# Decode attention over a cached context: the order of the last loads, the softmax's rearrangement, and the placing of results

## The chip, the cores and the metric

The kernel runs on one core of a Trainium2 chip. The metric is the device time of one execution in microseconds: the median over several runs of the program without a profiler. A profiled execution stands beside it and has a time of its own.

## The reference

Everything is float32. The input `x` is 8 tokens (one for each of 8 batches) of 512 channels. It is normalised once, and two branches are added to it:

```
x  = A_x;  xn = layernorm(x)
q  = (xn @ wq) -> 32 query heads of 128        # wq 512 x 4096
k, v = caches [8 batches, 8 kv heads, 8192, 128]; 4 query heads share one kv head
A  = softmax(q k^T / sqrt(128)) v -> 4096 columns, @ wo      # wo 4096 x 512
u  = gelu(layernorm(xn)[b, d] * w1[f] + b1[f])               # f = 0..1791
B  = sum over f of u * w2[f], + b2
out = x + A + B
```

Each of the two caches holds 64 pairs of batch and kv head with 8192 x 128 numbers, 4 MiB a pair, so 512 MiB are read once and meet only 4 query rows each.

## The kernel before, in words

Work runs in 64 steps, `i = h * 8 + b`: kv head `h` outside, batch `b` inside. For every step one tile of keys and one of values is loaded, each 128 partitions x 64 rows x 128 channels (partition `p` holds the context rows `64p` to `64p + 63`). All loads go through one queue (SP, L86) into a ring of 5 such tiles (`RING`); a load is issued in `load_next`, called where a tile has been used up: after the scores of keys (`qk`, L261) and after the last part of values (`pv`, L337). The order of the loads is a list sorted by hand-made keys: keys of step `i` at `2i`, values of step `i` at `2(i + LAG) + 1` with `LAG = 2`. Near the end that gives keys 62, values 60, keys 63, values 61, values 62, values 63. The very last tile comes in six pieces.

The engines take their work in the order in which the program is written. The loop runs over `i`, and in one pass three steps are under way:

- keys `i` are turned in place by VectorE in four quarters (`turn_keys`, L247, 32 x 32 blocks);
- step `k = i - 1` has its scores made by TensorE (`qk`, L258) against `Z`, which holds the queries of one head, placed in blocks (`q_place`, L241; two copies of `Z`, filled by 14 copies on ScalarE), and then its softmax: row maximum (`sm_max`, L268), its spread to all partitions (`sm_spread`, L273), bias (`sm_bias`, L279), exponential with row sums (`sm_exp`, L285), 32 x 32 transposition (`sm_turn`, L291), the sum's reciprocal (`sm_sum`, L298 and L300), and seven matmuls of 64 columns with four ScalarE copies that put the probabilities as weights into `PT` (`sm_place`, L309 and L313);
- step `v = i - 2` multiplies its values with `PT` (`pv`, L327; four parts; 512 columns to a matmul, four strips of 32 output rows), two parts ahead of the softmax's end of step `k` and two behind it. The result is scaled on its way out of PSUM (L340), and one pass later `o_place` gathers it (L355 to L359; in the last head L363 and L365) into `OT`. The last step's values (`FINE`) go in matmuls of 128 columns (L333), so that each piece can start when it has landed.

After a head is complete, `o_project` multiplies with `wo` (L371) and adds to `yacc`, which is kept as four quarters of 32 partitions. The Mixer branch (`mx_begin`, `mx_step`, `mx_end`) runs beside it: for each batch 14 Gelus on ScalarE, with a product and a sum on GpSimd, two a pass in seven passes of every eight.

The rings in PSUM: `misc` has three buffers, the score and result tiles four, the Mixer one.

Of the kernel before, what the change touches and what calls it, by code (L numbers as in the profile page):

```python
# [15 lines left out]
REP = HQ // HKV  # L16
# [6 lines left out]
GT = CH_T // NB  # L23
# [7 lines left out]
ZW = (2 * NB - 1) * RB  # L31
NS = 2 * NB - 1
SL = CH_T * REP
FINE = N_IT - 1
LAG = 2
RING = 5
PAD = 384
# [3 lines left out]
def attn_mixer_kernel(ctx: ExitStack, tc: tile.TileContext, x, kc, vc, wq, wo, w1, b1, w2, b2, out):  # L41
# [7 lines left out]
    t2k = ctx.enter_context(tc.tile_pool(name="t2k", bufs=3))  # L49
# [17 lines left out]
    order.sort(key=lambda o: -o[0])  # L67
    WQ = []
# [8 lines left out]
    def load_next():  # L77
        if order:
            _, src, to, i = order.pop()
            h, b = divmod(i, B)  # L80
            t = ring.tile([P, NT, DH], F32, name="raw")
            rows = src[b, h].rearrange("(p t) d -> p t d", p=P)
            first, last = to is KR and not i, not order
            at = 0
            for n in (CH_T,) * NCH if first else (CH_T, CH_T, CH_T, 2 * GT, GT, GT) if last else (NT,):
                nc.sync.dma_start(t[:, at:at + n, :], rows[:, at:at + n, :])  # L86
                at += n
            to[i] = t
# [10 lines left out]
    x_sb = t2k.tile([B, D], F32, name="t2k")  # L99
# [4 lines left out]
    b2t = const.tile([B, 1], F32, name="b2t")  # L104
    yacc = const.tile([P, D // NB], F32, name="yacc")
    nc.vector.memset(yacc, 0.0)
# [13 lines left out]
    oh = const.tile([P, REP], F32, name="oh")  # L120
    nc.vector.tensor_reduce(oh, ident.rearrange("p (g h) -> p h g", h=REP), AX.X, ALU.add)
    ohw = t2k.tile([P, P], F32, name="t2k")
# [4 lines left out]
    oh32 = t2k.tile([P, W], F32, name="t2k")  # L127
# [3 lines left out]
    oh2 = work.tile([P, REP], F32, name="oh2")  # L131
# [5 lines left out]
    turn = const.tile([P, NS * W], F32, name="turn")  # L137
    for y in range(NS):
        o = -y % NB * W
        nc.vector.tensor_copy(turn[:, y * W:(y + 1) * W], ident[:, o:o + W])  # L140
# [15 lines left out]
    spread = const.tile([B, W], F32, name="spread")  # L156
    nc.vector.memset(spread, 0.0)
    nc.vector.tensor_copy(spread.rearrange("b (c s) -> b c s", s=BS)[:, :, 0], ident[:B, :B])
    Z = []
    for k in range(2):  # L160
        z = const.tile([P, NB, B, ZW], F32, name=f"z{k}")
        nc.gpsimd.memset(z, 0.0)
        Z.append(z)
    PT = []
    for k in range(2):
        t = const.tile([P, NCH * SL + W - REP], F32, name=f"pt{k}")
        nc.gpsimd.memset(t, 0.0)
        PT.append(t)
# [18 lines left out]
    xn = t2k.tile([B, D], F32, name="t2k")  # L187
    layer_norm(xn, x_sb)
    hn = one.tile([B, D], F32, name="g")
# [3 lines left out]
    xnT = one.tile([P, NC, W], F32, name="sq")  # L193
    nc.vector.memset(xnT, 0.0)
    hnT = const.tile([P, NC, B], F32, name="hnT")
# [4 lines left out]
    for c in range(NC):  # L200
        nc.tensor.transpose(m[:, P + c * B:P + (c + 1) * B], hn[:, c * P:(c + 1) * P], ident[:B, :B])
    nc.vector.tensor_copy(hnT, m[:, P:P + NC * B].rearrange("p (c b) -> p c b", b=B))
    m = misc()
    for j in range(NB):
        nc.tensor.matmul(m[j * W:(j + 1) * W, :D // NB], spread, yx[:, quarter[j]], start=True, stop=True)
    nc.vector.tensor_copy(yacc, m[:, :D // NB])
# [4 lines left out]
    def q_project():  # L211
        for a in range(2):
            m = misc()
            for g in range(HKV // 2):
                for c in range(NC):
# [7 lines left out]
            for g in range(HKV // 2):  # L223
                nc.tensor.transpose(mt[:, g * P:(g + 1) * P], q[:, g * DH:(g + 1) * DH], ident)
            nc.vector.tensor_copy(QT[:, a * HKV // 2:(a + 1) * HKV // 2].rearrange("p g b r -> p g r b"),
                                  mt.rearrange("p (g r b) -> p g r b", r=REP, b=W)[:, :, :, :B])
        WQ.clear()
        load_next()
        load_next()

    def q_place(h):
# [5 lines left out]
        dst = Z[h % 2].rearrange("p q b (s k r) -> p (q b) s k r", k=2, r=REP)  # L237
        for s in range(2 * NB - 1):
            a = slice(s % NB * W, (s % NB + 1) * W)
            for k in range(2):  # L240
                nc.scalar.copy(dst[a, :, s, k, :], src[a])  # L241
# [9 lines left out]
    def qk(i):  # L251
# [3 lines left out]
        for q in range(NB):  # L255
            for c in range(NCH):
                o = -c % NB * RB
                nc.tensor.matmul(S[i][c * W:(c + 1) * W, :].rearrange("p (t j) -> p t j", j=W),  # L258
                                 Z[h % 2][:, q, b, o:o + W], k[:, c * CH_T:(c + 1) * CH_T, q * W:(q + 1) * W],
# [16 lines left out]
    def sm_bias(i):  # L276
        t = one.tile([P, P], F32, name="sq")
# [3 lines left out]

    def sm_exp(i):
        p = big()
        lr = work.tile([P, 1], F32, name="lr")
# [3 lines left out]
    def sm_turn(i):  # L288
        p, lr = st[i]
        t = big()  # L290
        nc.vector.transpose(t, p)  # L291
        st[i] = (t, lr)

    RL = {}

    def sm_sum(i):
        m = misc()
        nc.tensor.matmul(m[:, :1], ohl, st[i][1], start=True, stop=True)  # L298
        rl = work.tile([P, 1], F32, name="rl")
        nc.vector.reciprocal(rl, m[:, :1])  # L300
        RL[i] = rl

    def sm_place(i):
        t = st.pop(i)[0].rearrange("p (t r x) -> p r t x", r=NB, x=RB)
        m = misc()
        for v in range(NS):
            r = v % NB
            o = -r % NB * W
            nc.tensor.matmul(m[:, v * SL:(v + 1) * SL].rearrange("p (t h) -> p t h", h=REP),  # L309
                             turn[:, o:o + P], t[:, r, :, :REP], start=True, stop=True)  # L310
        for a in range(NB):
            x = slice(a * W, (a + 1) * W)
            nc.scalar.copy(PT[i % 2][x, :NCH * SL], m[x, a * SL:(a + NCH) * SL])  # L313

# [3 lines left out]
    def pv(i, c):  # L318
        if not 0 <= i < N_IT:
            return  # L320
        if c == 0:
            O[i] = ps_a.tile([P, 512], F32, name="acc")
        v = VR[i][:, c * CH_T:(c + 1) * CH_T, :].rearrange("p t d -> p (t d)")
        for j in range(NB):
            o = (c * NB + j) * GT * REP
            if i < FINE:
                nc.tensor.matmul(O[i][j * W:(j + 1) * W, :], PT[i % 2][:, o:o + W], v[:, j * 512:(j + 1) * 512],  # L327
                                 start=(c == 0), stop=(c == NCH - 1))
                continue
            for u in range(GT):  # L330
                w = PT[i % 2][:, o + u * REP:o + u * REP + W]
                x = slice((j * GT + u) * DH, (j * GT + u + 1) * DH)
                nc.tensor.matmul(O[i][u * W:(u + 1) * W, :DH], w, v[:, x],  # L333
                                 start=(c == 0 and j == 0), stop=(c == NCH - 1 and j == NB - 1))
        if c == NCH - 1:
            del VR[i]
            load_next()  # L337
            w = 512 if i < FINE else DH
            ob = big()
            nc.scalar.activation(ob[:, :w], O.pop(i)[:, :w], AF.Copy, scale=RL.pop(i))  # L340
            OB[i] = ob
# [3 lines left out]
    def o_place(i):  # L345
        if not 0 <= i < N_IT:
            return
        h, b = divmod(i, B)
        if b == 0:
            OT[h] = OTS[h % 2]  # L350
        m = misc()
        ob = OB.pop(i)
        if h < HKV - 1:
            for u in range(GT):
                nc.tensor.matmul(m[:, :DH], pick[:, u, :], ob[:, u * DH:(u + 1) * DH],  # L355
                                 start=(u == 0), stop=(u == GT - 1))
            t = one.tile([P, P], F32, name="sq")
            nc.vector.tensor_tensor(t, m[:, :DH], keep, op=ALU.mult)
            nc.vector.tensor_reduce(OT[h][:, :, BS * b], t.rearrange("p (g c) -> p c g", c=REP), AX.X, ALU.add)  # L359
            return  # L360
        n = GT if i < FINE else 1
# [5 lines left out]
    def o_project(h):  # L367
        m = misc()
        for r in range(REP):
# [4 lines left out]


    mx = {}

    def mx_begin(b):
        hb = ps_h.tile([P, D], F32, name="hb")
        for c in range(NC):  # L380
            nc.tensor.matmul(hb[:, c * P:(c + 1) * P], hnT[:, c, b:b + 1].to_broadcast([P, P]), ident, start=True, stop=True)
# [11 lines left out]
    def mx_end(b):  # L393
        m = misc()
        for j in range(NB):
            nc.tensor.matmul(m[j * W:(j + 1) * W, :D // NB], bsel[:, BO - BS * b:BO - BS * b + W], mx[b][1][:, quarter[j]],
                             start=True, stop=True)
        nc.vector.tensor_add(yacc, m[:, :D // NB], yacc)
# [3 lines left out]
    q_place(0)  # L402
    for i in range(N_IT + LAG + 1):
        h, b = divmod(i, B)
        k, v = i - 1, i - LAG
        soft = 0 <= k < N_IT
        turn_keys(i, 0)
        o_place(v - 1)
        if soft:
            qk(k)  # L410
        turn_keys(i, 1)
        if soft:
            sm_max(k)
            sm_spread(k)
        if h and b == 0:
            mx_end(h - 1)
        if h < HKV:
            if b == 0:
                mx_begin(h)
            else:  # L420
                mx_step(h, 2 * (b - 1))
# [50 lines left out]
```

## Time and profile before

| | us |
|---|---|
| median of 3 runs | 1307.39 (1307.25 to 1311.2) |
| profiled execution | 1319.94 |
| its span in the trace | 1318.2 |
| PE busy | 939.2 (71%) |
| DVE busy | 728.1 (55%) |
| ACT busy | 463.5 (35%) |
| POOL busy | 232.2 (18%) |
| mean granted TensorE clock | 0.81 of full |

Busy times add up what an engine's instructions took; they overlap between engines. PE is TensorE with its matmuls, PEld its weight loads, DVE VectorE, ACT ScalarE, POOL GpSimd, SP the queue that issues the loads. A row of the groups names the line, the engine, the operation, what it writes and reads, the count, busy time and mean of one, and behind the bar the engine's idle time ahead of them with what ended it. One matmul in float32 leaves two records, so the 16 matmuls that multiply one step's values are 32 records.

### The profile page before, as it was taken

How to read it: one execution, taken by the hardware profiler on the slowest of the kernel's cores; microseconds unless marked ns; L12 is line 12 of the kernel's file. 1: busy time of each engine (PE TensorE's matmuls, PEld its weight loads, DVE VectorE, ACT ScalarE, POOL GpSimd, SP SyncE). 2: the span in 40 equal slices, each digit the busy share in tenths (PEclk: the TensorE clock that was granted, in tenths of full speed). 3: DMA queues.
4: the chain of work that ended last, by engine and by line, in shares of the span. 5: the costliest groups of instructions: out<-in, count | busy, mean ns of one | idle time of the engine just before them, and what ended most of it. 6: DMA issues, size and time to landing. Idle time of an engine off the chain costs nothing.

```text
span 1318.2 us, 15548 instructions
## 1 busy us (share of the span) xinstructions
PE 939.2 (71%) x6578; PEld 431.0 (33%) x6578; DVE 728.1 (55%) x751; ACT 463.5 (35%) x805; POOL 232.2 (18%) x248
## 2 busy tenths in 40 slices
PE   3677676786668677786667677687587677686777
PEld 3233233332233233342223233243243233233334
DVE  3765654655654646655655645655646645654530
ACT  0343333343334332343333433343323433333331
POOL 2111211221121211221111211111201221121210
PEclk9887897778886778778887877877868887887777
DMA  9999999999999999999999999999999999999990
GB/s 399 438 433 430 429 433 436 432 430 429 434 433 436 429 429 433 436 430 432 434 429 434 432 433 431 432 433 433 433 430 430 434 436 431 430 430 434 434 405 32
DMA packets 21656, 554.69 MB, mean 421 GB/s; under 512 B 2476, under 2 KB 2508, under 8 KB 3412
## 3 DMA queue, kind: packets, MB, share of 16 engines
q1 hardware_dynamic: 21444, 553.67, 97.6%
q8 instruction: 51, 0.84, 0.2%
q14 instruction: 17, 0.14, 0.0%
q10 hardware_dynamic: 16, 0.02, 0.0%
q0 software_dynamic: 128, 0.02, 0.0%
HBM read 553.69 MB, written 0.02 MB: 420 GB/s over the span
## 4 chain that ended last, share of the span: by engine, by line
DMA 61%; PE 31%; DVE 6%; ACT 1%; issue 0%; SPq 0%; ACTq 0%
DMA raw<-in_A_v_cache_dram 59%; PE acc L327 16%; PE misc L309 8%; DVE raw L247 5%; PE acc L258 4%; DMA raw<-in_A_wq_dram 2%; PE misc L355 1%; PE misc L298 1%; PE misc L218 1%; DVE mr L268 1%; DVE t2k L291 1%; ACT t2k L340 1%; PE acc L333 0%; PE misc L363 0%; DVE sq L279 0%
## 5 line engine op out<-in xcount | busy, mean ns | idle before, releaser
L247 DVE STREAM_TRANSPOSE raw<-raw 128x2048 f32<-128x2048 f32 x256 | 589.1, 2304 | 314.4 <-DMA raw<-in_A_k_cache_dram 314.4
L327 PE MATMUL acc<-raw,pt 128*32 128x512 f32 x2016 | 361.2, 853 | 149.7 <-DMA raw<-in_A_v_cache_dram 149.7
L390 POOL TENSOR_SCALAR g<-g,w2t 128x512 f32<-128x512 f32 x112 | 77.9, 695 | 1011.1 <-ACT g L389 1011.1
L258 PE MATMUL acc<-raw,z 128*32 128x512 f32 x2048 | 248.7, 622 | 4.3 <-DVE raw L247 2.3
L313 ACT COPY pt<-misc 32x256 f32<-32x256 f32 x256 | 93.0, 363 | 308.7 <-PE misc L309 306.4
L285 ACT ACT_TABLE_LOAD x64 | 82.1, 1283 | 315.5 <-DVE nb L279 315.5
L327 PEld LDWEIGHTS acc<-raw,pt 128*32 128x32 f32 x2016 | 68.1, 138 | 292.5 <-issue 206.8
L309 PE MATMUL misc<-t2k,turn 128*128 128x64 f32 x896 | 153.1, 340 | 10.0 <-DVE rl L300 7.8
L309 PEld LDWEIGHTS misc<-t2k,turn 128*128 128x128 f32 x896 | 145.3, 252 | 11.8 <-DVE rl L300 5.8
L391 POOL TENSOR_TENSOR macc<-macc,g 128x512 f32<-128x512 f32 x112 | 143.0, 1277 | 9.3
L389 ACT ACTIVATE g<-hb,b1t,w1t 128x512 f32<-128x512 f32 x112 | 87.2, 778 | 91.0 <-POOL macc L391 90.0
L273 PE MATMUL misc<-ident,mr 128*128 128x128 f32 x128 | 33.1, 342 | 112.9 <-DVE mr L268 112.0
L258 PEld LDWEIGHTS acc<-raw,z 128*32 128x32 f32 x2048 | 62.7, 114 | 139.8 <-issue 127.7
L355 PE MATMUL misc<-t2k,pick 128*128 128x128 f32 x448 | 71.2, 307 | 37.7 <-ACT t2k L340 37.7
L355 PEld LDWEIGHTS misc<-t2k,pick 128*128 128x128 f32 x448 | 60.0, 208 | 88.5 <-ACT t2k L340 87.9
L389 ACT ACT_TABLE_LOAD x64 | 82.1, 1283 | 1.2
L273 PEld LDWEIGHTS misc<-ident,mr 128*128 128x128 f32 x128 | 20.2, 198 | 171.2 <-DVE mr L268 171.2
L340 ACT ACTIVATE t2k<-acc,rl 128x512 f32<-128x512 f32 x64 | 43.7, 682 | 89.8 <-PE acc L327 81.7
L300 DVE RECIPROCAL rl<-misc 128x1 f32<-128x1 f32 x64 | 9.9, 154 | 107.2 <-PE misc L298 107.2
L298 PEld LDWEIGHTS misc<-lr,ohl 128*128 128x128 f32 x128 | 25.5, 249 | 120.1 <-issue 64.8
L268 DVE TENSOR_REDUCE mr<-acc 128x1 f32<-128x512 f32 x64 | 42.9, 670 | 34.3 <-PE acc L258 34.1
L298 PE MATMUL misc<-lr,ohl 128*128 128x1 f32 x128 | 31.0, 311 | 33.5 <-ACT t2k L285 33.5
(79 smaller groups left out, 335.3 us busy)
## 6 DMA issues: line engine op xcount, KB each, us to landing
raw<-in_A_k_cache_dram SPq DMA_DIRECT2D x63, 4096.0 KB, 35.0
raw<-in_A_v_cache_dram SPq DMA_DIRECT2D x63, 4096.0 KB, 31.0
raw<-in_A_wq_dram SPq DMA_DIRECT2D x2, 4096.0 KB, 17.0
wo<-in_A_wo_dram SPq DMA_DIRECT2D x8, 1024.0 KB, 31.2
raw<-in_A_k_cache_dram SPq DMA_DIRECT2D x4, 1024.0 KB, 28.5
raw<-in_A_v_cache_dram SPq DMA_DIRECT2D x3, 1024.0 KB, 26.6
raw<-in_A_v_cache_dram SPq DMA_DIRECT2D x1, 512.0 KB
raw<-in_A_v_cache_dram SPq DMA_DIRECT2D x2, 256.0 KB, 29.3
```

The lines of the kernel that those rows point to most:

```text
L247: nc.vector.transpose(k, k)
L258: nc.tensor.matmul(S[i][c * W:(c + 1) * W, :].rearrange("p (t j) -> p t j", j=W), Z[h % 2][:, q, b, o:o + W], k[:, c * CH_T:(c + 1) * CH_T ...
L285: nc.scalar.activation(p, S.pop(i), AF.Exp, bias=st[i], scale=SCALE, accum_out=lr)
L298: nc.tensor.matmul(m[:, :1], ohl, st[i][1], start=True, stop=True)
L309: nc.tensor.matmul(m[:, v * SL:(v + 1) * SL].rearrange("p (t h) -> p t h", h=REP), turn[:, o:o + P], t[:, r, :, :REP], start=True, stop=True)
L313: nc.scalar.copy(PT[i % 2][x, :NCH * SL], m[x, a * SL:(a + NCH) * SL])
L327: nc.tensor.matmul(O[i][j * W:(j + 1) * W, :], PT[i % 2][:, o:o + W], v[:, j * 512:(j + 1) * 512], start=(c == 0), stop=(c == NCH - 1))
L340: nc.scalar.activation(ob[:, :w], O.pop(i)[:, :w], AF.Copy, scale=RL.pop(i))
L355: nc.tensor.matmul(m[:, :DH], pick[:, u, :], ob[:, u * DH:(u + 1) * DH], start=(u == 0), stop=(u == GT - 1))
L389: nc.scalar.activation(g, hb, AF.Gelu_apprx_tanh, bias=b1t[:, j:j + 1], scale=w1t[:, j:j + 1])
L390: nc.gpsimd.tensor_scalar(g, g, w2t[:, j:j + 1], 1.0, op0=ALU.mult, op1=ALU.mult)
L391: nc.gpsimd.tensor_add(acc, acc, g)
```

## The change

It moves keys 63 one place forward in the list of loads, ahead of values 60, and leaves out the values in pass 62 (values 60 move to pass 63, 61 to the end), so that scores and softmax of step 63 stand ahead of values 61. `sm_place`'s seven matmuls and four copies become one matmul of 512 columns with a permutation matrix (`send`), and the 32 x 32 transposition comes after it, from PSUM straight into `PT`. The rows of `PT` and the columns of `v` are taken in another order to suit. Results of four batches are collected in one tile and placed together (not in the last head). The projections of queries and outputs, the Mixer's start and its end use matmuls 512 wide; `yacc` is made from `yrow` ahead of the last head. `Z` has one copy and 8 instead of 14 copies to fill it. The Mixer's steps run in every pass from the first on, without the empty one in eight.

```
@@ the order of loads
     order.sort(key=lambda o: -o[0])
+    at = [o[1:] for o in order].index((kc, KR, N_IT - 1))
+    order[at], order[at + 1] = order[at + 1], order[at]
@@ q_project
-            for g in range(HKV // 2):
-                for c in range(NC):
-                    for r in range(REP):
-                        o = ((a * HKV // 2 + g) * REP + r) * DH
-                        nc.tensor.matmul(m[r * W:(r + 1) * W, g * DH:(g + 1) * DH], xnT[:, c, :],
-                                         WQ[c][:, o:o + DH], start=(c == 0), stop=(c == NC - 1))
+            for c in range(NC):
+                for g in range(HKV // 2):
+                    o = (a * HKV // 2 + g) * REP * DH
+                    nc.tensor.matmul(m[g * W:(g + 1) * W, :], xnT[:, c, :], WQ[c][:, o:o + REP * DH],
+                                     start=(c == 0), stop=(c == NC - 1))
...
@@ softmax
+    def sm_send(i):
+        p, lr = st[i]
+        m = misc()
+        nc.tensor.matmul(m, send, p, start=True, stop=True)
+        st[i] = m
+        h, b = divmod(i, B)
+        if h == HKV - 1:
+            ms = misc()
+            nc.tensor.matmul(ms[:, :1], ohl, lr, start=True, stop=True)
+            st[i] = (m, ms)
     def sm_turn(i):
-        p, lr = st[i]
-        t = big()
-        nc.vector.transpose(t, p)
-        st[i] = (t, lr)
...
-        for v in range(NS):
-            r = v % NB
-            o = -r % NB * W
-            nc.tensor.matmul(m[:, v * SL:(v + 1) * SL].rearrange("p (t h) -> p t h", h=REP),
-                             turn[:, o:o + P], t[:, r, :, :REP], start=True, stop=True)
-        for a in range(NB):
-            x = slice(a * W, (a + 1) * W)
-            nc.scalar.copy(PT[i % 2][x, :NCH * SL], m[x, a * SL:(a + NCH) * SL])
+        m = st.pop(i)
+        if i >= N_IT - B:
+            m, ms = m
+            RL[i] = small.tile([P, 1], F32, name="rl")
+            nc.vector.reciprocal(RL[i], ms[:, :1])
+        nc.vector.transpose(PT[i % NPT][:, :CH_T * W], m)
@@ pv, all but the last step
+            v = VR[i].rearrange("p (c t) d -> p t c d", c=NCH)
+            for t in range(part * CH_T // 2, (part + 1) * CH_T // 2):
+                j = t % NB
+                nc.tensor.matmul(O[i][j * W:(j + 1) * W, :].rearrange("p (c d) -> p c d", c=NCH),
+                                 pt[:, t * W:(t + 1) * W], v[:, t], start=(t < NB), stop=(t >= CH_T - NB))
...
@@ o_place, all but the last head: only after every fourth batch
+            for c in range(NCH):
+                nc.tensor.matmul(m.rearrange("p (b d) -> p b d", b=HB), pick[:, c, :], ob[:, :, c * DH:(c + 1) * DH],
+                                 start=(c == 0), stop=(c == NCH - 1))
...
@@ the loop
+    def pair(i):
+        h, b = divmod(i, B)
+        k = i - 1
+        late = i == N_IT - 1
+        v = i - LAG - late if i != N_IT - LAG else -1
+        mb, mj = divmod(2 * (i - 1), NF)
+        mixing = 0 <= mb < B
+        turn_keys(i, 0)
+        if v > 0:
+            o_place(v - 1)
+        if k >= 0:
+            qk(k)
+        if b == 0:
+            q_place(h)
+        turn_keys(i, 1)
+        if k >= 0:
+            sm_max(k)
+            sm_spread(k)
+        if mixing:
+            if mj == 0:
+                if mb:
+                    mx_end(mb - 1)
+                mx_begin(mb)
+            mx_step(mb, mj)
+        if mb == B and mj == 0:
+            mx_end(B - 1)
+        turn_keys(i, 2)
+        if k >= 0:
+            sm_bias(k)
+            sm_exp(k)
+        if v >= 0:
+            pv(v, 0)
+        turn_keys(i, 3)
+        if k >= 0:
+            sm_send(k)
+        if v >= 0 and late:
+            pv(v, 1)
+        if k >= 0:
+            sm_turn(k)
+        if v >= 0 and not late:
+            pv(v, 1)
+        if mixing:
+            mx_step(mb, mj + 1)
...
+    for i in range(N_IT):
+        pair(i)
+    k = N_IT - 1
+    v = k - LAG
+    qk(k)
+    o_place(v - 1)
+    sm_max(k)
+    sm_spread(k)
+    sm_bias(k)
+    sm_exp(k)
+    sm_send(k)
+    values(v)
+    sm_turn(k)
+    o_place(v)
+    for v in range(v + 1, N_IT):
+        if v < FINE:
+            values(v)
+        else:
+            at = 0
+            for n in PIECES:
+                pv(v, (at, at + n))
+                at += n
+        o_place(v)
+    o_project(HKV - 1)
```

`values(v)` is `pv(v, 0)` and `pv(v, 1)`; `PIECES` are the same six pieces (16, 16, 16, 8, 4, 4 rows of 64) as before.

More of the change, by code (lines that the diff above doesn't have):

```diff
@@ L84, in load_next @@
             at = 0
[L85 removed]
+            for n in (CH_T,) * NCH if first else PIECES if last else (NT,):
                 nc.sync.dma_start(t[:, at:at + n, :], rows[:, at:at + n, :])
@@ L199, in attn_mixer_kernel @@
     nc.vector.tensor_copy(xnT[:, :, :B], m[:, :NC * B].rearrange("p (c b) -> p c b", b=B))
[L200 to L202 removed]
     m = misc()
[L204 to L206 removed]
+    nc.tensor.matmul(m[:W, :], spread, yx, start=True, stop=True)
+    nc.vector.tensor_copy(yrow, m[:W, :])
     QT = const.tile([P, HKV, B, REP], F32, name="qt")
@@ L316, in attn_mixer_kernel @@
-    O, OB = {}, {}
-    def pv(i, c):
-        if not 0 <= i < N_IT:
-            return
[L321 to L341, printed above, removed]
+    RL = {}
@@ new lines, in attn_mixer_kernel, with pv @@
+    O, OB = {}, {}
+    def pv(i, part):
+        h, b = divmod(i, B)
+        pt = PT[i % NPT]
+        if i < FINE:
+            first, last = part == 0, part == 1
+            if first:
+                O[i] = ps_a.tile([P, 512], F32, name="acc")
+            v = VR[i].rearrange("p (c t) d -> p t c d", c=NCH)
[4 more added lines that the diff above has]
+        else:
+            first, last = part[0] == 0, part[1] == NT
+            if first:
+                O[i] = ps_a.tile([P, 512], F32, name="acc")
+            for n in range(*part):
+                c, t = divmod(n, CH_T)
+                j = n % NB
+                o = t * W + c * REP
+                nc.tensor.matmul(O[i][j * W:(j + 1) * W, :DH], pt[:, o:o + W], VR[i][:, n, :],
+                                 start=(n < NB), stop=(n >= NT - NB))
+        if not last:
+            return
+        del VR[i]
+        load_next()
+        if h < HKV - 1:
+            if b % HB == 0:
+                OB[h] = one.tile([P, HB, 512], F32, name="ob")
+            nc.scalar.copy(OB[h][:, b % HB, :], O.pop(i))
+            return
+        w = 512 if i < FINE else DH
+        ob = big()
+        nc.scalar.activation(ob[:, :w], O.pop(i)[:, :w], AF.Copy, scale=RL.pop(i))
+        OB[i] = ob
@@ L368, in o_project @@
         m = misc()
+        if h < HKV - 1:
+            for r in range(REP):
+                nc.tensor.matmul(m[:W, :], OT[h][:, r, :], wos[h][:, r, :], start=(r == 0), stop=(r == REP - 1))
+            nc.vector.tensor_add(yrow, m[:W, :], yrow)
+            return
         for r in range(REP):
@@ L373, in o_project, with y_quarters @@
         nc.vector.tensor_add(yacc, m[:, :D // NB], yacc)
+    def y_quarters():
+        m = misc()
+        for j in range(NB):
+            nc.tensor.matmul(m[j * W:(j + 1) * W, :D // NB], ident[:W, :W], yrow[:, quarter[j]], start=True, stop=True)
+        nc.vector.tensor_copy(yacc, m[:, :D // NB])
     mx = {}
@@ L394, in mx_end @@
         m = misc()
[L395 to L398, printed above, removed]
+        nc.tensor.matmul(m[:W, :], bsel[:, BO - BS * b:BO - BS * b + W], mx[b][1], start=True, stop=True)
+        nc.vector.tensor_add(yrow, m[:W, :], yrow)
     q_project()
-    q_place(0)
-    for i in range(N_IT + LAG + 1):
+    def pair(i):
```

160 lines of the change are left out of this document (69 added, 91 removed).

## The prediction

> **What bounds the kernel now.** I read the page first: the span, the slices of DMA, the transfers.
>
> ```profile
> span 1318.2 us, 15548 instructions
> ...
> DMA  9999999999999999999999999999999999999990
> ...
> DMA packets 21656, 554.69 MB, mean 421 GB/s; under 512 B 2476, under 2 KB 2508, under 8 KB 3412
> ...
> raw<-in_A_k_cache_dram SPq DMA_DIRECT2D x63, 4096.0 KB, 35.0
> raw<-in_A_v_cache_dram SPq DMA_DIRECT2D x63, 4096.0 KB, 31.0
> ```
>
> The digit of DMA is 9 in every slice but the last: the caches stream without a hole, and the last slice of 33 us has almost no transfers. To see whether the stream has slack, the table of stretches (busy PE, PEld, DVE, ACT, POOL; then clock, DMA share, GB/s), one row for the middle and fine ones for the end:
>
> ```profile
> 1040.00:1240.00 200.00, 143.15 (x938) 64.06 (x941) 111.29 (x109) 69.90 (x119) 36.04 (x37) 0.79 1.00 432
> 1240.00:1244.00 4.00, 3.13 (x17) 0.44 (x9) 2.25 (x1) 1.78 (x5) 0.00 (x0) 0.62 1.08 467
> 1244.00:1248.00 4.00, 4.00 (x40) 1.87 (x40) 2.44 (x3) 1.99 (x2) 1.82 (x2) 1.00 0.93 401
> 1276.00:1280.00 4.00, 4.00 (x23) 3.66 (x24) 0.17 (x1) 0.32 (x1) 0.00 (x0) 0.50 0.96 410
> 1284.00:1288.00 4.00, 3.92 (x20) 2.38 (x24) 0.17 (x1) 2.09 (x3) 1.70 (x2) 0.50 0.58 238
> 1288.00:1292.00 4.00, 3.97 (x24) 0.72 (x16) 0.00 (x0) 0.00 (x0) 0.27 (x1) 0.64 0.27 101
> 1292.00:1296.00 4.00, 2.56 (x26) 0.94 (x26) 1.19 (x4) 1.69 (x2) 0.00 (x0) 1.00 0.00 0
> ```
>
> The two hundred microseconds from 1040 read share 1.00 and 432 GB/s, and the slices before them show no other picture: up to about 1276 the transfers set the time and no engine does. One load of 4096 KB (4.19 MB) takes 4.19/0.432 = 9.7 us, and the page's 35.0 and 31.0 us from issue to landing mean that about three loads are always outstanding. The last byte lands at about 1291. The span ends at 1318.2, so some 27 us are work after the stream. The chain in order of time (start, length, what) says what that work is:
>
> ```profile
> 1272.40 3.64 PE acc L327 x16
> 1276.04 0.52 PE misc L298 x2
> 1276.55 3.09 PE misc L309 x14
> 1279.64 3.62 PE acc L327 x16
> ...
> 1284.08 1.87 PE misc L363 x8
> 1285.95 6.07 PE acc L258 x32
> ...
> 1292.05 0.70 DVE mr L268
> ...
> 1294.30 1.28 ACT L285
> ...
> 1295.59 0.79 ACT t2k L285 x2
> ...
> 1297.26 2.83 PE misc L309 x14
> 1300.10 3.62 PE acc L327 x16
> ...
> 1304.54 1.87 PE misc L363 x8
> 1306.40 6.10 PE acc L333 x128
> ```
>
> PE works in program order: values 61 (L327), then the scores of the last keys (L258), their softmax (L268, L285, L309), the second half of values 62, and values 63 in small pieces (L333). The keys had long been there; their scores queue behind values 61, which came after them. The transfers and their landings, from the timeline:
>
> ```profile
> 1241.75 2.31 DVE L247 STREAM_TRANSPOSE raw<-raw 128x2048 f32<-128x2048 f32 x1 [5.48 <-DMA raw<-in_A_k_cache_dram]
> ...
> 1244.94 3.64 PE L258 MATMUL acc<-raw,z 128*32 128x512 f32 x32
> ...
> 1251.54 1.92 PE L327 MATMUL acc<-raw,pt 128*32 128x512 f32 x16 [1.65 <-DMA raw<-in_A_v_cache_dram]
> ...
> 1262.62 2.31 DVE L247 STREAM_TRANSPOSE raw<-raw 128x2048 f32<-128x2048 f32 x1 [7.92 <-DMA raw<-in_A_k_cache_dram]
> ...
> 1272.40 3.64 PE L327 MATMUL acc<-raw,pt 128*32 128x512 f32 x16 [4.09 <-DMA raw<-in_A_v_cache_dram]
> ```
>
> and the issues of the SP queue alone, in a narrower stretch of the same view:
>
> ```profile
> 1259.84 0.81 SPq L86 DMA_DIRECT2D raw<-in_A_v_cache_dram  x2
> ```
>
> So keys 62 landed at 1241.7, values 60 at 1251.5, keys 63 at 1262.6, values 61 at 1272.3, and the first pieces of values 63 were issued at 1259.8; values 62 then land near 1282 and 63 near 1291. These rows also give both prices of each block: 32 records of L258 take 3.64 us at clock 1.00 and 6.07 mostly at 0.50; 16 of L327 take 1.92 or 3.64.
>
> **The change, part by part.** In the middle of the kernel these groups bear on it (busy us and mean ns of one, then idle time and its releaser):
>
> ```profile
> L247 DVE STREAM_TRANSPOSE raw<-raw 128x2048 f32<-128x2048 f32 x256 | 589.1, 2304 | 314.4 <-DMA raw<-in_A_k_cache_dram 314.4
> ...
> L309 PE MATMUL misc<-t2k,turn 128*128 128x64 f32 x896 | 153.1, 340 | 10.0 <-DVE rl L300 7.8 <-DVE t2k L291 2.2
> ...
> L313 ACT COPY pt<-misc 32x256 f32<-32x256 f32 x256 | 93.0, 363 | 308.7 <-PE misc L309 306.4
> ...
> L355 PE MATMUL misc<-t2k,pick 128*128 128x128 f32 x448 | 71.2, 307 | 37.7 <-ACT t2k L340 37.7
> ...
> L291 DVE STREAM_TRANSPOSE t2k<-t2k 128x512 f32<-128x512 f32 x64 | 45.5, 711 | 2.2 <-ACT t2k L285 2.2
> ...
> L241 ACT COPY z<-misc 32x128 f32<-32x128 f32 x112 | 23.2, 253 | 2.2 <-PE misc L234 1.6
> ```
>
> *One permutation matmul.* It removes 153.1/64 = 2.4 us of PE (L309) and 93.0/64 = 1.5 us of ACT (L313) a step. It adds one matmul 512 wide over the full array and moves the transpose behind it, reading PSUM. No row is this matmul. Above it stand four L355 matmuls of 128 columns (8 records x 307 = 2.5 us if laid end to end), below it an eighth of a half of values (1.92/8 = 0.24 warm). Four strips run side by side in L327, so two of its rounds take 1.92: one full matmul is 0.96 warm, 1.8 cold. I take these. The transpose was 0.71 from SBUF; L247 has 2.304/4 = 0.58 for as many columns, and twice 0.71 is a far end; I take 0.71. Its wait for PE moves DVE's next four key transposes back, exactly where the reciprocal of L300 stood in that queue: DVE still idles 314.4/64 = 4.9 us a step for keys. All of this lies under the stream: worth 0. Without that cover it would be 2 to 3 us a step, in favour.
>
> *Four batches placed together.* The same columns pass PE (4 x 512 instead of 16 x 128), DVE's product and sum are four times as long and a quarter as many. Zero, under the stream; the last head keeps the old form, so the tail doesn't see it. *One Z buffer*: 8 copies of 0.253, 2.0 us, instead of 14, between the scores of two steps 19 us apart. Zero; without cover 2 us a head, 16 in all. *Wide projections*: the query projection stands before the stream's first release, with three loads queued behind it; the others run once a head. Zero, with 2 us either way without cover. *Mixer on every step*: POOL and ACT work is only moved; it ends at step 57, so Gelu no longer shares the tail, and the 1.28 us of table load before the last exponential goes.
>
> *Last keys one load sooner.* SP's queue now has keys 63 before values 60. Keys 63 are released by the step that released values 60 and the reverse, so both issue on time. Values 63 now wait for the scores of keys 62 (about 1259 by the rows: keys 62 from 1241.7, four transposes of 2.3 with the row maximum of the step before between them, to about 1255, then 3.64) instead of values 60 done (1259.8). Three loads are outstanding then; no hole. The stream's end stays at 1291, with a bound of 2 us either way.
>
> New tail: keys 63 land at 1251.5 and are transposed by about 1266 (behind the softmax of 62 on DVE); values 60 land at 1262.6. PE then has: values 60 first half 3.6 (cold after its wait), the permutation of 62 at 1.8, second half 1.9: 1270. Scores 63: 3.6, to 1273.6; softmax 63 without the table load: 0.70 maximum, some 0.8 for spread and bias, 0.79 exponential and hand-overs, 3.2 in all: 1276.8. Permutation 1.0, values 61 3.8 (landed 1272.3): 1281.6. Copy 0.9 and placement 1.1: 1283.6, values 62 3.8: 1287.4, copy and placement: 1289.4. The pieces of values 63 follow the landings; the last four tiles finish about 0.4 after 1291.3: 1291.7. After the last piece the old order stays: from L333's end at 1306.40 + 6.10 = 1312.50 to 1318.2 is 5.7. Span 1297.4; I say 1298. Against 1318.2 that is 20 us.
>
> All at clock 0.50 the same list gives: 1262.6 + 3.6 + 1.8 + 3.6 + 6.1 + 3.2 + 1.8 + 7.3 + 2.8 + 7.3 + 2.8 + 6.1 + 5.7 = 1314.7, only 3.5 less.
>
> Which clock? In the rows, 3.6 us of L327 alone ended with the clock going from 0.62 to 1.00 at 1243; but from 1272 to 1290 PE was busy nearly throughout at 0.50, L309, gaps and L363 among it, until a whole L258 block had run. So long rows of 512-wide matmuls raise it; 64-wide and 4-wide ones between do not. The new tail loses L309 and starts with 10 us of wide ones, so I take 1.00 from about 1268. The Trainium skill ("TensorE: Matmul & The Clock Gate", Part 1: The HAM clock gate) has the clock rise after about 3.4 us of sustained activity. By that rule the old tail would have been fast from about 1276; the rows show 0.50 until 1290, so busy time is not what counts here. For the new tail rule and rows give the same 1298.
>
> **From the profile to the runs.** The profiled execution took 1319.94, span 1318.2 plus 1.7; the median of the runs is 1307.39, 12.5 lower. If the runs' stream is that much quicker and the tail alike, the change gives 1307.4 - 20 = 1287. If instead the runs' old tail had a better clock and their stream is the profile's, the new time is 1298 + 1.7 = 1300. At clock 1.00 the old tail's listed blocks would lose 1.7 + 0.2 + 1.4 + 1.7 + 0.8 + 2.4 + 1.1 + 1.7 + 0.8 + 3.0 = 14.8, so that is possible in full. I take the middle, 1293. The Trainium skill ("DMA: Bandwidth & Descriptors", Specifications) puts the fabric's ceiling at 435 GB/s; an estimate by it, 554.69/0.435 = 1275 against 1284 at 432, allows the stream 9 of the 12.5, which would make 1291.
>
> **The rivals.**
> *The gap lies wholly in the old tail's clock (part of my forecast's side, its small end):* 1300, faster by 7. For it: both rows above show clock 0.50 for most of the tail. Against: three runs within 4 us of one another, while a tail of varying clock would scatter.
> *Cold new tail:* the waits for values 60 and the softmax keep PE at 0.50. Span 1306 to 1315, that is 1295 to 1302 if the old tail of the runs was cold too, and 1308 to 1316 against a warm one: around no change, 1304 to 1311. For it: the 0.50 of the old tail. Against: the rise at 1243.
> *Last values bind anyway:* the stream's end is later, because values 63 are issued later; the tail then follows it by 6. It needs scores 62 later than about 1275 to cost anything, against 1259; price one for one.
> *Slower:* DVE's queue. Its transpose of the softmax now waits for PE's permutation, which sits behind half of values that wait for their landing; the next keys' transposes are behind it. From 4.9 us more a step (transpose and wait together) keys are released late, the outstanding loads shrink, and each further microsecond costs 63 over the run: half a microsecond past that point, less the 14 of the tail, gives 1307.4 + 31 - 14 = 1324. For it: DVE is in order. Against: the reciprocal stood there too, with the same wait.
>
> **How the numbers follow.** Forecast (warm new tail, 1287 to 1299) 0.62; the tail's clock explains all, 1299 to 1303: 0.2; cold new tail, no change 0.11; binding last values, 1304 to 1311: 0.02; slower 0.05. What a measurement of this kernel tells from no change is 0.3%, 3.9 us: faster below 1303.5 is 0.82, same 0.13, slower 0.05. Predicted 1293; the range 1284 to 1303 goes from 1287 less the stream's 2 us bound and rounding to the edge of the second case.
>
> **What would show it.** In the profile after: keys 63 transposed ahead of the arrival of values 60; L258's last block before values 61 on PE; the last transfers again at about 1290, and a span ending 6 to 8 us behind them; share 1.00 and 432 GB/s in the middle; no table load in the last softmax. A tail at clock 0.50, a middle with a share below 1.00, or transfers ending late would make the prediction wrong.

## The result, and the profile after

The changed kernel takes 1297.62 us (median of 6 runs, 1297.27 to 1299.58), the kernel before 1309.38 (6 runs, 1307.25 to 1311.86). The ratio is 0.9912, with a 95% interval of 0.9895 to 0.9929: 11.8 us faster. Of the six runs before, three took about 1307.4 us and three about 1311.6; against these the change is worth 9.8 and 14.0. The profiled execution took 1299.58, its span is 1297.8.

The page of the changed kernel, the lines that answer to those of before:

```profile
span 1297.8 us, 11840 instructions
...
DMA  9999999999999999999999999999999999999996
...
DMA packets 21642, 554.47 MB, mean 427 GB/s; under 512 B 2477, under 2 KB 2509, under 8 KB 3413
```

The stream is as dense as before and now reaches nearly to the end of the span. The stretches (PE, PEld, DVE, ACT, POOL busy; clock; DMA share; GB/s):

```profile
1040.00:1240.00 200.00, 130.37 (x790) 40.01 (x785) 110.91 (x100) 37.61 (x59) 21.38 (x22) 0.82 1.00 432
```
```profile
1268.00:1272.00 4.00, 3.15 (x30) 1.62 (x22) 0.76 (x2) 0.00 (x0) 0.00 (x0) 1.00 0.90 385
1272.00:1276.00 4.00, 2.63 (x10) 1.38 (x13) 0.39 (x3) 0.78 (x2) 0.00 (x0) 0.55 0.96 412
1276.00:1280.00 4.00, 4.00 (x24) 0.83 (x20) 0.07 (x1) 0.00 (x0) 0.00 (x0) 0.60 0.98 413
1280.00:1284.00 4.00, 3.18 (x32) 1.51 (x28) 0.88 (x2) 0.69 (x1) 0.00 (x0) 1.00 0.79 329
1284.00:1288.00 4.00, 3.13 (x30) 1.11 (x22) 0.00 (x0) 0.69 (x1) 0.00 (x0) 1.00 0.50 202
1288.00:1292.00 4.00, 4.00 (x133) 3.81 (x132) 0.17 (x1) 0.00 (x0) 0.00 (x0) 1.00 0.06 18
```

In the middle PE is busy for 130 us of 200 instead of 143, ACT for 38 instead of 70 (partly because the Mixer ends sooner), and the stream still reads 1.00 and 432. At the end the transfers of the loads stop at 1289.0; before they stopped at about 1291.5. Two stretches of before, then one of after:

```profile
1290.00:1291.00 1.00, 1.00 (x12) 0.26 (x8) 0.00 (x0) 0.00 (x0) 0.00 (x0) 0.57 0.13 51
1291.00:1292.00 1.00, 0.97 (x12) 0.06 (x4) 0.00 (x0) 0.00 (x0) 0.00 (x0) 1.00 0.03 10
```
```profile
1289.00:1290.00 1.00, 1.00 (x48) 1.00 (x40) 0.00 (x0) 0.00 (x0) 0.00 (x0) 1.00 0.00 0
```

The chain in order of time:

```profile
1263.35 1.13 PE misc L295 x2
1264.48 0.12 PE misc L300 x2
1264.59 1.85 PE acc L324 x16
1266.45 3.43 PE acc L255 x32
1269.88 1.00 PE misc L381 x8
...
1273.58 2.07 PE misc L295 x2
1275.65 0.22 PE misc L300 x2
1275.87 5.28 PE acc L324 x32
...
1281.91 1.06 PE misc L381 x8
1282.97 3.61 PE acc L324 x32
...
1287.41 1.06 PE misc L381 x8
1288.46 3.67 PE acc L334 x128
```

L255 is the scores of the last keys (L258 before), L295 the permutation, L324 values, L334 the last values in pieces. Scores 63 start at 1266.4 instead of 1285.9, the last values at 1288.5 instead of 1306.4. The last byte lands while they run, and the span ends about 9 us behind it instead of 27.

### The profile page after: what moved, and what is told of

Its sections match the earlier page's. It is cut to its first block, busy times and chain, and to the rows that moved or that the text cites. A ratio compares the mean times of both kernels' runs of the same rounds, so it can differ in the third digit from the quotient of the medians.

```text
span 1297.8 us, 11840 instructions
## 1 busy us (share of the span) xinstructions
PE 848.7 (65%) x4932; PEld 248.3 (19%) x4932; DVE 717.9 (55%) x633; ACT 337.6 (26%) x487; POOL 229.8 (18%) x247
## 4 chain that ended last, share of the span: by engine, by line
DMA 75%; PE 21%; DVE 2%; issue 1%; ACT 1%; SPq 0%; ACTq 0%; DVEq 0%
DMA raw<-in_A_v_cache_dram 65%; PE acc L324 12%; DMA raw<-in_A_k_cache_dram 9%; PE misc L295 4%; PE acc L255 2%; DMA raw<-in_A_wq_dram 2%; DVE raw L245 2%; PE misc L216 1%; PE misc L389 1%; PE misc L381 0%; PE misc L423 0%; PE acc L334 0%; ACT t2k L287 0%; DVE mr L265 0%; PE hb L409 0%
## 5 line engine op out<-in xcount | busy, mean ns | idle before, releaser
L324 PE MATMUL acc<-raw,pt 128*32 128x512 f32 x2016 | 341.5, 811 | 177.2 <-DMA raw<-in_A_v_cache_dram 177.2
L255 PE MATMUL acc<-raw,z 128*32 128x512 f32 x2048 | 247.0, 606 | 3.5 <-ACT z L239 2.0
L270 PE MATMUL misc<-ident,mr 128*128 128x128 f32 x128 | 40.8, 412 | 228.5 <-DVE mr L265 228.5
L309 DVE STREAM_TRANSPOSE pt<-misc 128x512 f32<-128x512 f32 x64 | 45.8, 715 | 238.8 <-PE misc L295 231.9
L324 PEld LDWEIGHTS acc<-raw,pt 128*32 128x32 f32 x2016 | 67.8, 133 | 374.5 <-issue 340.3
L343 ACT COPY ob<-acc 128x512 f32<-128x512 f32 x56 | 32.8, 586 | 358.1 <-PE acc L324 358.1
L295 PE MATMUL misc<-t2k,send 128*128 128x512 f32 x128 | 98.2, 857 | 7.8 <-ACT t2k L287 7.7
L255 PEld LDWEIGHTS acc<-raw,z 128*32 128x32 f32 x2048 | 65.9, 111 | 166.1 <-issue 160.1
L287 ACT ACTIVATE t2k<-acc,nb 128x512 f32<-128x512 f32 x64 | 44.0, 687 | 150.3 <-DVE nb L276 149.8
L366 PE MATMUL misc<-ob,pick 128*128 128x512 f32 x112 | 51.8, 605 | 5.5 <-ACT ob L343 5.5
L295 PEld LDWEIGHTS misc<-t2k,send 128*128 128x128 f32 x128 | 27.2, 265 | 105.9 <-issue 86.1
L366 PEld LDWEIGHTS misc<-ob,pick 128*128 128x128 f32 x112 | 20.1, 189 | 26.8 <-issue 20.1
L389 PE MATMUL misc<-wo,ot 128*32 128x512 f32 x56 | 25.2, 592 | 0.0
```

The costliest lines, as they stand in the source:

```text
L270: nc.tensor.matmul(m[:, :P], st[i].to_broadcast([P, P]), ident, start=True, stop=True)
L287: nc.scalar.activation(p, S.pop(i), AF.Exp, bias=st[i], scale=SCALE, accum_out=lr)
L295: nc.tensor.matmul(m, send, p, start=True, stop=True)
L309: nc.vector.transpose(PT[i % NPT][:, :CH_T * W], m)
L324: nc.tensor.matmul(O[i][j * W:(j + 1) * W, :].rearrange("p (c d) -> p c d", c=NCH), pt[:, t * W:(t + 1) * W], v[:, t], start=(t < NB), sto ...
L366: nc.tensor.matmul(m.rearrange("p (b d) -> p b d", b=HB), pick[:, c, :], ob[:, :, c * DH:(c + 1) * DH], start=(c == 0), stop=(c == NCH - 1))
```

## The experiments

Theory A, to be tested: the end's order of work earns the gain, and all that the change does in the middle is hidden. Rival B: the permutation and the wide matmuls earn it. Theory D: the clock in the old end is part of it. (A letter can stand for another theory in a later expectation, which then says what it means.)

**The end alone, in the kernel before.** The list of loads is changed, and the end runs in the new order with the old softmax:

```
+    at = [o[1:] for o in order].index((kc, KR, N_IT - 1))
+    order[at], order[at + 1] = order[at + 1], order[at]
-    for i in range(N_IT + LAG + 1):
-        k, v = i - 1, i - LAG
+    for i in range(N_IT):
+        late = i == N_IT - 1
+        k, v = i - 1, i - LAG - late if i != N_IT - LAG else -1
...  # then: scores and softmax 63, values 61, placing 63, values 62, 63
```

> The kernel before with only its end changed: keys 63 load ahead of values 60, and the scores and softmax of step 63 stand ahead of values 61; the seven matmuls, four copies and everything else of the middle stay. Theory A (the whole gain is the end's order, the middle is hidden under the transfers): about 0.993 of before, some 1299 to 1301, since the new order's gain of about 12 us remains, less about 3 us for the seven 64-column matmuls and the table load that stay in the end. Rival B (the permutation matmul and the wide matmuls earn it, in the middle or in the end): within 0.3% of before, 1306 to 1311.

Measured: 1300.29 (7 runs), ratio 0.992 (0.9888 to 0.9951). Theory A's figure; B would have been 1306 or more. Its chain:

```profile
1264.86 26.96 DMA raw<-in_A_v_cache_dram
...
1291.86 0.47 PE acc L335 x8
```

The last piece waits for its landing at 1291.8, and the span ends at 1297.9, 6 us behind: this end is bound by the stream.

**All but the end.** The changed kernel without the exchange in the list, and with the old order of work in the last passes:

```
-    at = [o[1:] for o in order].index((kc, KR, N_IT - 1))
-    order[at], order[at + 1] = order[at + 1], order[at]
-        v = i - LAG - late if i != N_IT - LAG else -1
+        v = i - LAG
```

> The changed kernel with the end's order of before: values 60 load ahead of keys 63, values 60 in pass 62, 61 in pass 63, half of values 62 behind the softmax of step 63. All else as changed. Theory A: 1304 to 1308; the middle gives nothing, and only the shorter softmax in the end (2.4 us of 64-column matmuls less, no table load) and the clock gain a few microseconds on before. Rival B: 1297 to 1300, the changed kernel's time.

Measured: 1301.21 (9 runs), ratio 0.9928 (0.9903 to 0.9953). That is 3 us below what theory A gave it: by itself this half earns nearly as much as the other. A stretch and the chain show where:

```profile
1276.00:1284.00 8.00, 6.38 (x58) 2.36 (x50) 1.08 (x3) 0.69 (x1) 0.00 (x0) 1.00 0.88 369
```
```profile
1269.79 3.64 PE acc L322 x16
...
1278.75 3.62 PE acc L253 x32
...
1290.37 3.67 PE acc L332 x128
```

The clock is 1.00 from 1276 on. Scores 63 take 3.6 us instead of 6.1, the last values 3.7 instead of 6.1, and L309 and the table load are gone. Besides, the loads land sooner: values 61, for which PE waits, start at 1269.8 (first line of the chain) instead of 1272.4, and the last byte lands at 1289 instead of 1291.5. So theory A does not hold as it was put: the form of the softmax matters in the end, not only the order, and the new middle earns some 2.6 us through the landings. How the rest divides between the softmax and the clock no run shows.

**Keys not sooner.** The changed kernel without the two lines that exchange the loads.

> The changed kernel with one thing undone: keys 63 load behind values 60 again, as before; softmax 63 still ahead of values 61. If the earlier load is what lets the scores stand early (theory A): keys 63 land about 10 us later, near 1261, are turned by about 1271 to 1273 and their scores follow at about 1273 instead of 1266, so 3 to 6 us more than the changed kernel, 1301 to 1304. Rival C (only the place in PE's order counts, the load is early enough anyway): within 0.2% of the changed kernel, 1296 to 1300.

Measured: 1304.70 (12 runs). 7 us above the changed kernel, so the earlier load counts (rival C falls), and by more than was expected. VectorE's timeline:

```profile
1259.90 2.31 DVE L243 STREAM_TRANSPOSE raw<-raw 128x2048 f32<-128x2048 f32 x1 [7.86 <-DMA raw<-in_A_k_cache_dram]
...
1264.40 0.65 DVE L263 TENSOR_REDUCE mr<-acc 128x1 f32<-128x512 f32 x1
```

DVE stands 7.9 us for keys 63, and the row maximum of step 62 is queued behind their first two turns. With it the whole softmax of 62, and on PE values 60, are late. (7 us is against 1297.6, measured beside the kernel before in another series; the fastest run of the kernel before lay between 1307.0 and 1307.7 in every series.)

**Late keys, maximum first.** That variant, with maximum and bias of steps 61 and 62 moved ahead of the turns of the next keys:

```
+        first = i >= N_IT - LAG
-        turn_keys(i, 0)
+        if not first:
+            turn_keys(i, 0)
...  # likewise 1 and 2; for these passes they follow sm_exp(k)
```

> The variant with keys 63 behind values 60, and DVE's order changed in the last two passes: maximum, bias of steps 61 and 62 ahead of the turns of keys 62 and 63. Theory H (in that variant the late keys cost 7 us mostly because the maximum of step 62 queues on DVE behind their turns, and values 60 on PE behind that): values 60 start near their landing at 1251, scores 63 follow the last turn at about 1269 instead of 1272, 1300 to 1302.5. Rival I (the late landing alone costs it): 1304 to 1305.5, as without the change of order.

Measured: 1301.95 (9 runs), theory H's range. The chain now goes through the landing and the turns alone:

```profile
1259.75 8.90 DVE raw L243 x4
...
1268.70 4.12 PE acc L253 x26
```

So of the 7 us that the late load costs, about 3 are DVE's queue, and the rest is the landing.

**Keys sooner, old order of work.** The variant without the new end, with the exchange of loads put back.

> The changed kernel with keys 63 loading ahead of values 60 as changed, but the end's order of work as before (values 60 in pass 62, 61 in pass 63, scores 63 behind values 61). Theory A' (load and order only work together): values 60 now hold up PE ahead of scores 62, and scores 63 still queue behind values 61; about the time of the variant with neither, 1300 to 1304. Rival L (the sooner load alone earns the end's gain): the changed kernel's time, 1297 to 1299.

Measured: 1303.97 (7 runs). As theory A' had it:

```profile
1259.74 3.64 PE L324 MATMUL acc<-raw,pt 128*32 128x512 f32 x16 [13.42 <-DMA raw<-in_A_v_cache_dram]
```

PE stands 13.4 us for values 60, with scores 62 queued behind. The four cases in one line: neither 1301.2, sooner load alone 1304.0, new order alone 1304.7, both 1297.3 to 1297.6. Each half by itself costs 3 us, since it puts a wait for a landing ahead of work that is ready; together they save 4.

**Before, PE kept busy.** The kernel before with matmuls that nobody reads where PE pauses:

```
+        if i == N_IT - 1:
+            warm(4)          # 512 columns each
         pv(v, 0)
         pv(v, 1)
+        if i == N_IT:
+            warm(1)
```

> The kernel before with five matmuls of 512 columns added in the end, whose results nobody reads: four ahead of values 61, where PE waits for their landing, and one ahead of the last softmax's 64-column matmuls, where it waits for the exponential. Theory D (the old end runs at half clock because PE pauses before it, and that is why the profiled run and the runs differ by up to 12 us): clock 1.00 from values 61 on, and the time falls to 1303 to 1306 in spite of the added work. Rival E (the clock there is not set by these pauses): 4 to 8 us of added work behind the same clock, 1310 to 1318.

Measured: 1305.57 (12 runs), ratio 0.9964 (0.9943 to 0.9986), within theory D's range. Added work made it faster. Its chain has values 61 and scores 63 at full clock:

```profile
1272.59 1.92 PE acc L327 x16
...
1280.22 3.62 PE acc L258 x32
```

In the 27 runs of the kernel before beside this one, 11 took 1307.2 to 1308.4 us, 13 took 1310.9 to 1312.1 and 3 took 1320.2 to 1320.3. With the fillers eleven of 12 runs took 1305.2 to 1306.5, below all of these, and one 1309.2. So theory D holds: the old end's time depends on its clock, and the profile of before (1319.94) had caught the slowest of three levels. That the two other levels also come from where the clock rises fits, but is not shown: no trace has them, and of 42 further runs of the kernel before two, 1314.2 and 1315.6, lie between levels.

**Old work put back.** The changed kernel with the seven matmuls and four copies added in 56 steps, unread:

```
+        if i < N_IT - B:
+            extra, old = misc(), big()
+            for n in range(7):
+                nc.tensor.matmul(extra[:, n * 64:(n + 1) * 64], rep[:, n % NB, :], p[:, n * 64:(n + 1) * 64],
+                                 start=True, stop=True)
+            for g in range(NB):
+                nc.scalar.copy(old[g * W:(g + 1) * W, :256], extra[g * W:(g + 1) * W, :256])
```

> The changed kernel with the removed work put back beside the new: in the first 56 steps seven matmuls of 64 columns with full weights and four copies of 32x256 on ScalarE stand behind the permutation matmul; nobody reads their results. The end is untouched. Cover (theory A): the 2.4 us of PE and 1.5 us of ACT a step lie under the transfers and the time stays within 0.3% of the changed kernel, 1296 to 1301; at 32 more instructions a step the last byte may land about a microsecond later. Rival B (the middle's work counts): 56 steps by 2.4 us is 134 us more; even a tenth of that shows, 1310 or more.

Measured: 1298.54 (7 runs). By this trace the matmuls put back kept PE busy for 96 us (the expectation had reckoned 134, from the mean of before) and the copies ACT for 82:

```profile
L301 PE MATMUL misc<-t2k,rep 128*128 128x64 f32 x784 | 96.4, 276 | 0.0
```

They cost 0.9 to 1.3 us against the two series of the changed kernel: the engines' time in the middle is hidden, and B falls as far as it rests on that time. What they do cost is in the stream. Keys 62 landed at 1241.7 as in the kernel before, not at 1240.4 as in the changed one; the last byte landed at 1290, and the chain ends on it:

```profile
1290.40 0.47 PE acc L341 x8
```

**Maximum first, in the changed kernel.** The maximum of step 61 ahead of the turns of keys 62, three turns of keys 63 ahead of the maximum of 62.

> The changed kernel with DVE's order changed in the last two passes: the row maximum of step 61 stands ahead of the turns of keys 62 (for whose landing it waited from 1238 to 1245), and three of the four turns of keys 63 ahead of the maximum of step 62. If the end is a chain of PE and DVE since keys 62 (theory F): scores 63 begin 2 to 3 us sooner, values 61 are no longer late, and the end goes back to 6 us behind the last byte at about 1289, 1295 to 1296. Rival G (the last values and the clock set the end anyway): as the changed kernel, 1297 to 1299.

Measured: 1299.23 (6 runs). Theory F fell, and the time lies a little above rival G's range too: scores 62 did come sooner, but then PE stood waiting for values 60, and its clock was down when they came.

```profile
1259.79 3.64 PE L324 MATMUL acc<-raw,pt 128*32 128x512 f32 x16 [1.58 <-DMA raw<-in_A_v_cache_dram]
1263.36 2.08 PE L295 MATMUL misc<-t2k,send 128*128 128x512 f32 x2
```

In the changed kernel the slow scores of 62 ran until 1259.4, nearly up to values 60 (1260.55), which then took 1.85 to 1.92 a half. What was saved ahead of the landing was lost behind it.

**Fillers in the last softmax**, and the changed kernel once more beside it:

```
     o_place(v - 1)
+    warm()
     sm_max(k)
     sm_spread(k)
     sm_bias(k)
+    warm()
     sm_exp(k)
```

> The changed kernel with two matmuls of 512 columns added whose results nobody reads: one ahead of the spread of step 63's maximum and one ahead of its permutation, where PE pauses for DVE and ACT. Theory D (a pause with narrow matmuls around it lets the clock fall to 0.50 for values 61, 5.3 us instead of 3.6): clock 1.00 through values 61, last piece bound by its landing at about 1289 to 1290, end 6 us behind it, 1 to 2 us below the changed kernel where its clock fell and no change where it did not: 1296 to 1297.5 on the chip where the changed kernel has 1297.6 to 1298. Rival E: the fillers delay the softmax by up to a microsecond each and nothing else, 1298 to 1300.

> The changed kernel once more, unaltered, beside the other two on the same chip: 1297 to 1299, the profile's end with or without the fall of the clock in the last softmax.

Measured: 1297.72 (6 runs) with the fillers, 1297.29 (6 runs) without: no difference. In the trace with the fillers the clock stayed up (first row), in that without it fell to 0.58:

```profile
1272.00:1276.00 4.00, 3.50 (x28) 1.49 (x32) 0.17 (x1) 0.45 (x2) 0.00 (x0) 1.00 0.99 424
```
```profile
1272.00:1276.00 4.00, 3.96 (x16) 1.47 (x20) 0.17 (x1) 0.00 (x0) 0.00 (x0) 0.58 0.98 418
```

But with the clock up the last pieces wait for the stream, which ends at the same place. That the fillers hold the clock is not shown by this one pair: with the old work put back the last softmax has no filler and the same pauses, and its clock stayed up as well:

```profile
1272.00:1276.00 4.00, 2.12 (x11) 1.13 (x15) 0.93 (x4) 0.78 (x2) 0.00 (x0) 1.00 0.94 403
```

No variant beat the changed kernel.

**More instructions.** The last byte landed between 1291 and 1292 in the three traces with some 15,550 instructions and at 1289 in the eight with 11,840. The start of the stream does not make this difference: VectorE's wait for a tile of keys still ends at 627.4 in both kernels, later at 902.4 instead of 903.7 and at 1101.0 instead of 1103.6; the end alone, with the old middle, goes with the kernel before (1104.0). The changed kernel with 66 one-column memsets on GpSimd in each of 56 passes:

> The changed kernel with 66 one-column memsets on GpSimd added in each of the first 56 passes, 3696 instructions that move no data of the kernel: the count of the kernel before. In the three traces with 15.5 thousand instructions the last byte landed at 1291, in the three with 11.8 thousand at 1289. Theory J (the loads of instructions take the stream's time): the last byte lands near 1291 and the end follows, 1297.5 to 1299.5. Rival K (something else of the old middle slows the stream): the last byte stays at 1289, 1297 to 1298.

Measured: 1308.22 (10 runs), 10.7 us more. The stretches at the end, its queue of instruction loads (15 packets and 0.11 MB in the changed kernel), and the landing of keys 62:

```profile
1288.00:1292.00 4.00, 3.18 (x32) 1.40 (x28) 0.88 (x2) 0.69 (x1) 0.00 (x0) 1.00 0.11 46
1292.00:1296.00 4.00, 3.15 (x32) 0.74 (x24) 0.00 (x0) 0.69 (x1) 0.00 (x0) 1.00 0.06 27
1296.00:1300.00 4.00, 3.98 (x120) 3.97 (x124) 0.17 (x1) 0.00 (x0) 0.00 (x0) 1.00 0.07 25
```
```profile
q14 instruction: 43, 0.35, 0.1%
```
```profile
1251.15 4.51 DVE L245 STREAM_TRANSPOSE raw<-raw 128x2048 f32<-128x2048 f32 x2 [6.16 <-DMA raw<-in_A_k_cache_dram]
```

From 1289 to about 1299.5 a share of 0.06 to 0.07 is left, as of one of 16 engines, at 25 to 27 GB/s, a sixteenth of 432 (the next expectation says 1301; finer stretches show 1299.5). Keys 62 landed at 1251.15 instead of 1240.44, so the delay was there before the end. It grew through the run: the waits for keys end about 2 us later than in the changed kernel near 320, 5 near 620 and 8 near 910. So it looks as if one engine fell behind a little with every load. That is far more than either theory gave.

**Fewer, longer instructions**, for the same busy time of GpSimd: 24 products of 64 columns a pass.

> The changed kernel with 24 products of 64 columns on GpSimd in each of the first 56 passes, 1344 instructions where the variant with one-column memsets had 3696, for about as much busy time of GpSimd (some 300 us against 367). In that variant the transfers trailed off at 25 GB/s, one sixteenth of the stream, until about 1301 instead of 1289, 12 us for 3696 instructions. Theory J (loads of instructions, on one of the 16 DMA engines, make that engine late): 1344/3696 of 12 us, the last byte at about 1293, the time 1298 to 1302. Rival K (GpSimd's activity itself slows transfers): nearly the same delay as there, the last byte at 1298 or later, 1304 or more.

Measured: 1297.90 (4 runs), no change, with GpSimd busy for 393 us on these.

```profile
1288.00:1292.00 4.00, 3.21 (x106) 2.85 (x102) 0.17 (x1) 0.37 (x1) 0.00 (x0) 1.00 0.06 19
```
```profile
q14 instruction: 24, 0.20, 0.0%
```

The last byte is at 1289 again, and keys 62 landed at 1240.43. Rival K falls: it is not GpSimd's busy time. Theory J's proportion falls too: 0.09 MB more of instruction loads than in the changed kernel cost nothing, 0.24 MB more made the last byte 10.5 us late. At 27 GB/s one engine needs 8.9 us for 0.24 MB and 3.3 for 0.09, so an engine with some time in hand would explain the second but not all of the first. The kernel before loads 0.23 MB more than the changed one, 0.20 of it on another queue (q8), and is 2.5 us late, so there is no one price for a megabyte either. Which engine loads whose instructions no row shows, and no run separates loading them from executing so many; the cause stays open.

## Why the prediction was right, and where its sizes were off

*The middle worth nothing*: right for the engines' time, as the old work put back shows, and mis-sized for the stream. The prediction kept the stream's end at 1291, with 2 us either way; with the new middle it is 1289, and every landing near the end is 1.1 to 2.6 us sooner. This is what parts the end alone, whose last piece waits for its landing at 1291.8, from the changed kernel: 1300.3 against 1297.6. So some 2.6 us of the gain are the middle's. The permutation matmul took 1.12 us at clock 1.00 and 2.07 at 0.50 (forecast 0.96 and 1.8), the transposition from PSUM 0.715 (0.71):

```profile
L309 DVE STREAM_TRANSPOSE pt<-misc 128x512 f32<-128x512 f32 x64 | 45.8, 715 | 238.8 <-PE misc L295 231.9
```

*The end's order*: right in mechanism. That the span came out almost to the digit (1298 against 1297.8) is luck, for several terms were off and cancelled. Values 60 landed at about 1259.8 (the wait in the variant with the old order), not 1262.6, so scores 63 began at 1266.4, 3.6 us sooner than forecast. The stream ended at 1289, not 1291, and in this trace the last pieces did not follow their landings: they stood behind the placing on PE until 1288.5 and were done at 1292.1, where 1291.7 was forecast. And the clock was not 1.00 from 1268 to the end: it fell in the last softmax, so that values 61 took 5.3 us instead of 3.8 and the permutation 2.1 instead of 1.0, 2.6 in all. The pauses of PE there:

```profile
1271.72 0.49 PE L270 MATMUL misc<-ident,mr 128*128 128x128 f32 x2 [0.85 <-DVE mr L265]
1273.58 2.07 PE L295 MATMUL misc<-t2k,send 128*128 128x512 f32 x2 [1.37 <-ACT t2k L287]
```

The Trainium skill ("TensorE: Matmul & The Clock Gate", Part 1: The HAM clock gate) has the clock fall after an idle window of about 3.4 us. This trace does not agree: PE was busy for 3.15 of the 4 us from 1268 and for 2.63 of the next 4, its longest pause was 1.37 us, and the clock went from 1.00 to 0.55. Pauses of about a microsecond can do, then, but need not: the trace with the old work put back has the same two, 0.85 and 1.37 us, at clock 1.00.

*From the profile to the runs*: this step was mis-sized. The prediction split the 12.5 us between the profile of before and the median into stream and tail, half each, and came to 1293, 14.4 us below the 1307.39 it started from; the changed kernel came out 9.8 below it. The variant kept busy speaks for the tail's clock as the whole of the 12.5: the profiled execution was one of the slowest level. Nor is the stream of the runs quicker than the profile's, as far as traces go: the changed kernel's two, of executions of 1299.58 and 1297.59 us, both end it at 1289. The small end of the forecast, 1300, was the better figure; the earlier landings make up the rest. The half and half itself missed by 4.6 us.

*Rivals*: one figure is wrong as it stands: against a cold tail of before, the cold new tail gives 1295 to 1304 (1315 - 1318.2 + 1307.4), not to 1302; the chances do not hang on it. The cold new tail came in part, for 7 us instead of 30. The argument against a tail that explains the gap, that three runs stood within 4 us, was too weak: three runs had not met the third level. Last values did not bind in the profile of the changed kernel, but do with the fillers and with the old work put back. The slower case, DVE's queue in the middle, did not come; the same mechanism appeared in the end instead, in the variants whose keys or values land behind work that is ready.

What the prediction didn't weigh is that the end could be shortened in two ways that overlap. All but the order gives 1301.2, the order alone 1300.3, both together 1297.3 to 1297.6. Each alone meets a limit of its own: the first ends with PE's work, whose last piece is done at 1294.0, 5 us behind the last landing; the second ends 6 us behind a landing at 1291.8, which the old middle keeps late. The changed kernel ends 7 to 9 us behind its last landing.

## What to carry to other kernels

When a stream of loads bounds a kernel, price a change by what stands behind the last byte, and check each of the last steps for a wait for a landing that is queued ahead of work already able to run. Moving a load and moving the work that uses it are one change: here each alone cost 3 us and both together saved 4. Work that is hidden under a stream can still delay it: compare the landings, not only the share of busy time. Before a profiled execution is scaled to the runs, look whether its time is one of several levels, and at which clock its last stage ran.

## What the runs showed of the hardware that was not expected

Added matmuls made the kernel before 5 us faster (1305.6 against a median of 1310.9; 2 us against its fastest level): with PE's pauses filled, its last stage ran at clock 1.00, where the profile of before shows 0.50.

The pages of the profile count loads of instructions among the transfers of the 16 engines (q8 and q14). 3696 tiny instructions on an engine with time to spare cost 10.7 us, while 1344 longer ones cost nothing. The Trainium skill ("Runtime: NRT & Kernel Launch", Instruction fetch mechanics) calls the cost of loading the next block of instructions "mostly hidden". If loading them is what made the stream late here, it was not hidden, but came out as one late engine of 16 behind the loads; that it is the loading is argued, not shown. That the changed kernel's 3,700 fewer instructions brought the last byte from 1291.5 to 1289 agrees with it, with 1290 for the variant half way (13,653 instructions), but no run took instructions from PE alone.
